# The sums of the first product's x blocks: added by VectorE in place of DMA, with new times for steps of the first and second product

## The chip, the cores and the metric

The kernel runs on one core of a Trainium2 chip. The metric is the device time of one execution in microseconds (us); lower is better. One profiled execution stands behind all rows of the trace.

## The reference

```python
x = attention(q, k, v)                   # causal, 2 batches, 12 heads, 448 tokens, head size 64
h = x @ w_in                             # x: 896 x 768, w_in: 768 x 2048
g = s * maximum(h, 0) ** 2 + b
x2 = g @ w_out                           # 2048 x 768
gate = 1 / (1 + exp(-(x2 @ w_gate)))     # 768 x 1536
out = ((gate * (x2 @ w_val)) @ w_out2)   # 1536 x 768
```

The weights arrive as 64-bit floats, and are read as pairs of 32-bit words.

## The kernel before, in words

**Stages.** Attention runs first, pair of heads by pair of heads, and leaves x in `x_b`: for each of six blocks of 128 features (k) and each of two batches (h) a tile of 128 x 448 for the high half and one for the low half (float32 split into two values that TensorE multiplies; x is their sum). Then come the first product (`w_in`, 16 feature blocks f), the second (`w_out`), the gate and value products, and the last product. Every product is made of three matmuls for each block: high by high, high weight by low x, low weight by high x. They stand in that order in `mm3`, so the third matmul of a product is the first that needs the weight's low half.

**The first product** has two parts. Feature blocks 0 to 7 are plain (`fill`: 18 matmuls for one f and one h). Blocks 8 to 15 are taken in four groups of two by a scheme with seven products in place of eight (class `Seven`, `early7`): it multiplies sums of weight blocks (`ab`, `s12`, `s34`, `d`) by sums and differences of x's blocks (`t1` to `t4`). Those differences need x in float32. `halves_of(k0, h)` is three blocks of a buffer `r_b` of 128 x 1344 elements for one quarter of x; `X11`, `X12`, `X21`, `X22` name the quarters. Before the change a quarter's high half is copied there by a DMA on SyncE's queue (`x_copy`, line 587), and its low half is added by an accumulating DMA on GpSimd's queue (`x_add`, line 591). Then `x_sum` makes a difference on VectorE (lines 599 and 601), `x_high` its high half on ScalarE (line 608) and `x_low` its low half on VectorE (line 611).

**A weight's way.** `load_words` (line 76) loads one piece of 768 KB into one of two raw buffers, by SyncE's queue. `float_steps` turns the pairs of words into float32 in four steps: one on ScalarE (line 87), two short ones on VectorE (lines 89 and 92), a long one on VectorE (line 97) and another (line 101), after which the raw buffer is free for the load after the next. `halves` makes the high half on ScalarE (line 114) and the low half either on VectorE by a subtraction (line 120) or, with `adder`, by a negating copy on ScalarE (line 117) and an accumulating DMA on GpSimd's queue (line 118).

**Order.** The order of instructions on each engine is written out by hand: `at(t, what, ...)` puts a step into a plan at time t, and the plan is emitted in order of t. The times only set the order; each engine works in order and waits where its operands are not there. One unit of plan time is nine matmuls. The plan's marks are X (start of the first product, first half of feature 0 done early), XQ = X + 32 (start of the seven-product scheme), Y = XQ + 28 (start of the second product), M = Y + 32 and 0 (start of the gate and value products, Y + 64). `PLAIN_LEAD[f]` says how long before its use feature f's weights are converted; `X_AT` holds the times of the steps on x's blocks, `OWN_1` and `OWN_2` those of the weights' steps in the seven-product schemes, `AFFINE_AT` and `G_AT` those of the steps that make the second product's input, `lead` the advance of the second product's weights. The first five features' conversions are taken one step at a time by `step` from one generator, `splits`. The load of a unit of weights is planned right behind the step that frees its raw buffer (`gone`).

The steps around the change, as the plan has them before:

```python
for i, n in enumerate((1, 0, 3, 2)):
    at(X + 1.5 + 2.2 * i, x_copy, n)
    at(X + 1.5 + 2.2 * i, x_add, n)
X_AT = (10.4, 11.07, 11.55, 14.31, 15, 15.6, 16.2, 17.5, 19, 20.06, 24.14, 26.97)
```

Of the kernel before, what the change touches and what calls it, by code (L numbers as in the profile page):

```python
# [13 lines left out]
ALU = mybir.AluOpType  # L14
U32 = mybir.dt.uint32
P = 128
# [8 lines left out]
def body(ctx: ExitStack, tc: tile.TileContext, qk, vp, w_in, w_outa, w_outb, s, b, w_gate, w_val, w_out2a, w_out2b, outT):  # L25
# [79 lines left out]
    def halves(tt, out, adder=False, name="w", slot=None):  # L105

        if slot is None:
            slot = turn("w", SLOTS, (1, 3, 0, 4, 2))
        hi = wp.tile([P, U, P], F32R, tag=f"{slot}h", name=f"{name}hi")
        lo = wp.tile([P, U, P], F32R, tag=f"{slot}l", name=f"{name}lo")  # L110
        out += [hi, lo]
        nn = tt.shape[1]
        hif, lof = (x.rearrange("p k m -> p (k m)")[:, :nn] for x in (hi, lo))
        nc.scalar.activation(out=hif, in_=f32(tt), func=AF.Copy)  # L114
        yield "dve"
        if adder:
            nc.scalar.activation(out=lof, in_=f32(hif), func=AF.Copy, scale=-1.0)  # L117
            nc.gpsimd.dma_start(out=lof, in_=f32(tt), accum_op=ALU.add)  # L118
        else:
            nc.vector.tensor_tensor(out=lof, in0=f32(tt), in1=f32(hif), op=ALU.subtract)  # L120

    def split_steps(raw, n, out):

        t = []
        yield from float_steps(raw, n, t)
        yield "act"
        yield from halves(t[0][:, :n * P], out)

    def mm3(acc, unit, K, x, h):

# [184 lines left out]
    def fill(f, h, k0, k1):  # L315
# [3 lines left out]
        wh, wl = split[f]  # L319
        mm3(acc[f, h], (wh[:, k0:k1], wl[:, k0:k1], k0, k1), KC, at_x, h)  # L320

    def splits():

        raw = load_words(w_in[0], KC)
        yield "act"
        for f in range(EARLY):
            now, raw = raw, load_words(w_in[f + 1], KC) if f + 1 < EARLY else None
            yield from split_steps(now, KC, split[f])
            yield "act"

    steps = splits()
# [208 lines left out]
    at(X + 0.9, step)  # L540
    at(X + 1.75, step)

    PLAIN_LEAD = (-0.15, -2.69, 0.73, 0.91, 1.15, 2.21, 2.47, 3.38)

    def plain_at(f):
        return X + PER * f - PLAIN_LEAD[f]
# [20 lines left out]

    for f in range(PLAIN):
        if f >= EARLY:
            split.append(unit(w_in[f], KC, plain_at(f), f"w{(1, 0, 4)[f - EARLY]}", f > EARLY))  # L570
        for h in range(B):
            t = X + (f + h / B) * PER
            if f == 0 and h == 0:
                at(t + 1.0, fill, 0, 0, KC // 2, KC)
            else:
                at(t, fill, f, h, 0, KC)
            timed(
                t + PER / B, (0.02, relu, lambda f=f, h=h: acc[f, h][:, :S], f, h), (0.35, square, f, h),
            )
# [2 lines left out]
    def halves_of(k0, h):  # L582
        return mem["rb"][:, B * k0 + h:B * (k0 + KH):B]

    def x_copy(n):
        k0, h = KH * (n // B), n % B
        nc.sync.dma_start(out=halves_of(k0, h), in_=f32(x_b[:, B * k0 + h:B * (k0 + KH):B, 0]))

    def x_add(n):
        k0, h = KH * (n // B), n % B  # L590
        nc.gpsimd.dma_start(out=halves_of(k0, h), in_=f32(x_b[:, B * k0 + h:B * (k0 + KH):B, 1]), accum_op=ALU.add)

    X11, X12, X21, X22 = ((0, 0), (0, 1), (KH, 0), (KH, 1))

# [15 lines left out]
    def x_low(ty, src):  # L610
        nc.vector.tensor_tensor(out=t_blocks(ty, 1), in0=halves_of(*src), in1=f32(t_blocks(ty, 0)), op=ALU.subtract)

    for i, n in enumerate((1, 0, 3, 2)):
        at(X + 1.5 + 2.2 * i, x_copy, n)
        at(X + 1.5 + 2.2 * i, x_add, n)
    X_AT = (10.4, 11.07, 11.55, 14.31, 15, 15.6, 16.2, 17.5, 19, 20.06, 24.14, 26.97)
    timed(
        X, (X_AT[0], x_sum, X11, X11, X12, ALU.subtract, False), (X_AT[1], x_high, "t1", X11),
        (X_AT[2], x_low, "t1", X11),
        (X_AT[3], x_sum, X12, X22, X12, ALU.subtract, False), (X_AT[4], x_high, "t3", X12),  # L620
        (X_AT[5], x_sum, X22, X11, X22, ALU.subtract, True), (X_AT[6], x_high, "t2", X22),
# [144 lines left out]
            3: ((1.05, add_r, q, f1), (1.40, relu_square, f1)),  # L766
        }[i]

    OWN_1 = {q: dict(zip(("g", "ab", "v", "s", "s12", "s34"), ts)) for q, ts in enumerate((((-10.2, -9.6, -8.8, -8.2), (-6.9, -6.3), (-7.7, -7.2, -6.6, -6.0), (-4.62, -4.32, -3.6, -3.3), (-2.58, -2.1), (-1.77, -0.68)), ((-4.23, -3.55, -2.65, -2.13), (-1.22, -0.46), (-1.56, -1.14, -0.54, -0.02), (0.38, 0.68, 1.4, 1.7), (3.49, 3.97), (3.23, 4.32)), ((2.77, 3.45, 4.35, 4.87), (6.29, 6.54), (5.32, 5.74, 6.34, 6.86), (7.38, 7.68, 8.4, 8.7), (9.32, 9.8), (10.23, 11.32)), ((9.77, 10.45, 11.35, 11.62), (13.26, 13.54), (12.32, 12.74, 13.34, 13.86), (14.38, 14.68, 15.4, 15.7), (16.12, 16.6), (17.23, 18.32))))}
    early7 = Seven(  # L770
        XQ, seq1, lambda q: tuple(w_in[f] for f in features(q)), OWN_1,
        lambda q: (f"w{1 - q % 2}", "w2", f"w{3 + q % 2}"), lambda n: mem["s1"][:, n % 4], first_x, evacuate_1,
# [14 lines left out]
    def g_time(k):  # L787
        return Y + 2 * k - G_AT[k]

    AFFINE_AT = (12.8, 14.6, 16.2, 17.8, 18.31, 21.0, 22.02, 24.83)  # L790
    G_AT = (3.0, 3.0, 3.0, 3.0, 3.0, 3.0, 3.0, 3.0, 4.93, 3.0, 2.34, 2.73, 2.95, 3.03, 1.1, 3.0)
    for k in range(PLAIN):
        for h in range(B):
            at(XQ + AFFINE_AT[k] + 0.8 * h, affine, k, h)
# [24 lines left out]
            )  # L819

    def lead(n):
        return (0.0, 0.0, 0.0, 0.0, 0.0, 0.63, 1.0, 1.64, 2.89, 3.64, 4.25, 5.0, 5.75, 7.45, 8.2, 8.95, 8.56)[n]

    for u in range(PIECES):
        w2.append(unit(w_outa[u], U, Y + PER * u - lead(u), f"w{W2[u]}"))
# [151 lines left out]
    seq = [(i, q) for i, q in seq if q < NF2]  # L977
    seq[-4:-2] = seq[-3], seq[-4]

    OWN_2 = {q: dict(zip(("g", "ab", "v", "s", "s12", "s34"), ts)) for q, ts in enumerate((((-15.6, -15.2, -14.5, -13.9), (-10.65, -9.8), (-13.3, -12.9, -12.3, -11.7), (-5.25, -4.95, -4.3, -4.0), (-4.6, -3.6), (-2.18, -1.97)), ((-11, -10.6, -10, -9.4), (-1.75, -1.25), (-8.9, -8.5, -7.9, -7.3), (-2.1, -1.8, 0.3, 0.6), (4.1, 5.09), (2.65, 3.1)), ((-6.38, -5.98, -5.12, -4.94), (5.78, 6.54), (5.32, 5.74, 6.34, 6.86), (7.38, 7.68, 8.4, 8.7), (9.32, 9.8), (10.23, 11.32))))}  # L980
    ring = {}

    def ringed(i, q):
# [193 lines left out]
```

## Time and profile before

| | |
|---|---|
| median of 3 runs | 556.46 us (555.77 to 559.13) |
| profiled execution | 556.3 us |
| its span, first to last instruction | 554.4 us |
| PE busy | 541.6 us (98%) |
| DVE busy | 430.6 us (78%) |
| ACT busy | 358.4 us (65%) |
| POOL busy | 91.2 us (16%) |
| granted TensorE clock, mean | 0.999 of full speed |

PE is TensorE's matmuls, PEld its weight loads, DVE VectorE, ACT ScalarE, POOL GpSimd, SP SyncE. A busy share is taken over the whole span. In a timeline a row is one instruction, or several alike in a run (x2); the bracket says how long its engine was idle just before it and what ended that. Times in the rows count from the span's start.

### The profile page before, as it was taken

The page shows a single profiled execution, that of the slowest core. Times are in us where ns is not written, and L with a number is a line of the kernel's source. Part 1 is how long each engine was busy: PE and PEld are TensorE (multiplying, and loading weights), DVE is VectorE, ACT ScalarE, POOL GpSimd, SP SyncE. Part 2 cuts the span into 40 slices and gives each one's busy share as a digit, 9 for nine tenths or more (in the row PEclk, how much of TensorE's full clock was granted, in tenths as well). Part 3 has the DMA queues.
Part 4 walks back from the last instruction along what each step waited for, and adds up shares of the span by engine and source line. Part 5 has one row for each costly group of instructions (what it writes and reads, how often), then busy time and mean ns, then how long its engine had stood idle before and what let it go on. Part 6 is the DMA issues. An engine that isn't in the chain of part 4 may idle for free.

```text
span 554.4 us, 8357 instructions
## 1 busy us (share of the span) xinstructions
PE 541.6 (98%) x3032; PEld 479.7 (87%) x3033; DVE 430.6 (78%) x783; ACT 358.4 (65%) x675; POOL 91.2 (16%) x147
## 2 busy tenths in 40 slices
PE   7999999899899999999999999999999999999997
PEld 3667789789799899999999999999999999999996
DVE  6899875689885899987789788888888999895300
ACT  7989945488789958954436777766767674734200
POOL 3667512101111000000000211121121210000000
PEclk9999999999999999999999999999999999999999
DMA  7846039787977334254345658888888863336000
GB/s 260 306 135 214 31 114 314 149 211 214 220 175 184 81 118 159 96 161 143 113 158 159 135 118 200 195 205 215 209 200 214 214 173 115 113 115 213 34 33 35
DMA packets 26425, 89.41 MB, mean 161 GB/s; under 512 B 2960, under 2 KB 10000, under 8 KB 26384
## 3 DMA queue, kind: packets, MB, share of 16 engines
q1 hardware_dynamic: 17152, 68.69, 34.9%
q0 software_dynamic: 8800, 19.27, 21.2%
q10 hardware_dynamic: 432, 0.92, 0.5%
q8 instruction: 24, 0.39, 0.3%
q14 instruction: 17, 0.14, 0.1%
HBM read 64.10 MB, written 2.75 MB: 121 GB/s over the span
## 4 chain that ended last, share of the span: by engine, by line
PE 65%; DMA 1%; ACT 0%; issue 0%; ACTq 0%
PE acc L135 18%; PE bankA L719 16%; PE acc L817 11%; PE bankC L719 8%; PE acc L1079 8%; PE bankE L719 4%; DMA d_w<-wt 1%; ACT ot L1092 0%; ACTq L1092 0%
## 5 line engine op out<-in xcount | busy, mean ns | idle before, releaser
L135 PE MATMUL acc<-x_b,whi 128*128 128x448 f32 x288 | 82.1, 366 | 0.9 <-ACT whi L114 0.9
L87 ACT ACTIVATE wt<-raw 128x768 f32<-128x768 f32 (+1 forms) x69 | 61.4, 890 | 24.0 <-DMA raw<-in_w_outb 8.2
L101 DVE SCALAR_TENSOR_TENSOR wt<-raw,wt 128x768 uint32<-128x768 uint32 (+1 forms) x69 | 65.6, 951 | 1.7
L97 DVE SCALAR_TENSOR_TENSOR wt<-raw,wt 128x768 uint32<-128x768 uint32 (+1 forms) x69 | 65.6, 950 | 1.3
L114 ACT ACTIVATE whi<-wt 128x768 fp32r<-128x768 f32 (+1 forms) x37 | 30.6, 826 | 44.1 <-DVE wt L101 41.1
L135 PEld LDWEIGHTS acc<-x_b,whi 128*128 128x128 f32 x288 | 53.9, 188 | 5.5 <-ACT whi L114 1.3
L89 DVE TENSOR_SCALAR wt<-wt 128x768 f32<-128x768 f32 (+1 forms) x69 | 38.6, 560 | 20.9 <-ACT wt L87 20.3
L135 PE MATMUL acc<-x_b,wlo 128*128 128x448 f32 x144 | 52.8, 367 | 1.8 <-DVE wlo L120 1.3
L213 ACT ACTIVATE pt<-pt,m 128x320 f32<-128x320 f32 (+6 forms) x84 | 41.7, 501 | 5.4 <-DVE m L210 5.3
L252 POOL TENSOR_SCALAR pt<-pt,r 128x128 f32<-128x128 f32 (+6 forms) x82 | 40.1, 510 | 27.7 <-DVE r L247 21.2
L120 DVE TENSOR_TENSOR wlo<-wt,whi 128x768 fp32r<-128x768 f32 (+1 forms) x35 | 33.1, 946 | 10.0 <-ACT whi L114 9.6
L92 DVE TENSOR_SCALAR wt<-wt 128x768 uint32<-128x768 uint32 (+1 forms) x69 | 38.5, 558 | 2.4
L118 POOL DMA_DIRECT2D ab_lo<-wt x16 | 13.8, 863 | 152.8 <-ACT ab_lo L117 118.5
L210 DVE CUSTOM_DVE_ANT_0 pt<-sc,mask 128x320 f32<-128x320 f32 (+6 forms) x84 | 30.4, 413 | 3.7 <-PE sc L223 3.4
L120 DVE TENSOR_TENSOR s_lo<-s,s_hi 128x768 fp32r<-128x768 f32 x16 | 15.3, 957 | 21.2 <-ACT s_hi L114 21.2
L135 PEld LDWEIGHTS acc<-x_b,wlo 128*128 128x128 f32 x144 | 27.0, 188 | 4.6 <-DVE wlo L120 1.7
L1092 ACT ACTIVATE ot<-acc 128x448 f32<-128x448 f32 x12 | 6.6, 546 | 36.2 <-PE acc L135 30.2
L114 ACT ACTIVATE s_hi<-s 128x768 fp32r<-128x768 f32 x32 | 26.7, 837 | 3.3 <-DVE s L661 3.3
L223 PE MATMUL sc<-qk 64*64 64x256 f32 (+6 forms) x336 | 24.9, 391 | 2.2 <-DMA qk<-in_qk 2.0
L118 POOL DMA_DIRECT2D s_lo<-s x16 | 13.8, 860 | 76.8 <-DVE wt L97 43.3
L294 PEld LDWEIGHTS po<-ptT,vt 128*64 128x64 f32 x192 | 12.6, 136 | 13.0 <-issue 9.4
L672 POOL DMA_DIRECT2D d_w<-wt x16 | 14.3, 897 | 57.9 <-ACT d_w L671 37.6
(214 smaller groups left out, 1433.5 us busy)
## 6 DMA issues: line engine op xcount, KB each, us to landing
raw<-in_w_in SPq DMA_DIRECT2D x16, 768.0 KB, 5.4
raw<-in_w_gate SPq DMA_DIRECT2D x12, 768.0 KB, 5.7
raw<-in_w_val SPq DMA_DIRECT2D x12, 768.0 KB, 5.9
ab_lo<-wt POOLq DMA_DIRECT2D x16, 384.0 KB, 5.7
s_lo<-s POOLq DMA_DIRECT2D x16, 384.0 KB, 4.8
raw<-in_w_outa SPq DMA_DIRECT2D x8, 768.0 KB, 4.2
qk<-in_qk SPq DMA_DIRECT2D x9, 608.0 KB, 5.1
raw<-in_w_out2a SPq DMA_DIRECT2D x6, 768.0 KB, 4.5
```

The costliest lines, as they stand in the source:

```text
L87: nc.scalar.activation(out=f32(tt), in_=f32(high), func=AF.Abs, scale=RAISE)
L89: nc.vector.tensor_scalar(out=f32(tt), in0=f32(tt), scalar1=F64_TINY, scalar2=F64_HUGE, op0=ALU.max, op1=ALU.min,)
L97: nc.vector.scalar_tensor_tensor(out=tt, in0=low, scalar=29, in1=tt, op0=ALU.logical_shift_right, op1=ALU.bitwise_or,)
L101: nc.vector.scalar_tensor_tensor(out=tt, in0=high, scalar=SIGN, in1=tt, op0=ALU.bitwise_and, op1=ALU.bitwise_xor,)
L114: nc.scalar.activation(out=hif, in_=f32(tt), func=AF.Copy)
L120: nc.vector.tensor_tensor(out=lof, in0=f32(tt), in1=f32(hif), op=ALU.subtract)
L135: nc.tensor.matmul(acc[:, :S], w[:, k - k0], m, start=k == 0 and i == 0, stop=k == K - 1 and i == 2)
L213: nc.scalar.activation(out=pc, in_=pc, func=AF.Exp, scale=-1.0, bias=m, accum_out=l)
L252: engine.tensor_scalar(out=probs(i, c), in0=probs(i, c), scalar1=st[i]["r"][:, c:c + 1], scalar2=1.0, op0=ALU.mult, op1=ALU.mult,)
L719: nc.tensor.matmul(acc[:, :S], a[:, j], m, start=fresh and j == 0 and n == 0, stop=j == KH - 1 and n == 2, skip_group_check=True,)
L817: nc.tensor.matmul(acc[:, :S], w[:, kk * GROUP + d], m, start=k == 0 and n == 0, stop=k == NF1 - 1 and n == 2,)
L1079: nc.tensor.matmul(acc[d, h][:, :S], w[:, k * GROUP + d], m, start=u == 0 and k == 0 and n == 0, stop=u == NF2 // 2 - 1 and k == 1 and n == 2,
```

## The change

`x_copy` and `x_add` go. In their place `x_whole` adds the two halves of a quarter of x on VectorE, at four times behind the others in `X_AT`. The other times of `X_AT` are set anew, most of them earlier. Feature 5's low half is now made with `adder` (`ADDED_EARLY`; features 6 and 7 had it before). `PLAIN_LEAD`, three entries of `OWN_1`, `AFFINE_AT`, `G_AT`, `lead` and three entries of `OWN_2` have new numbers.

```diff
--- before.py
+++ after.py
@@ -119,12 +119,12 @@
         else:
             nc.vector.tensor_tensor(out=lof, in0=f32(tt), in1=f32(hif), op=ALU.subtract)
 
-    def split_steps(raw, n, out):
+    def split_steps(raw, n, out, adder):
 
         t = []
         yield from float_steps(raw, n, t)
         yield "act"
-        yield from halves(t[0][:, :n * P], out)
+        yield from halves(t[0][:, :n * P], out, adder)
 
     def mm3(acc, unit, K, x, h):
 
@@ -319,13 +319,15 @@
         wh, wl = split[f]
         mm3(acc[f, h], (wh[:, k0:k1], wl[:, k0:k1], k0, k1), KC, at_x, h)
 
+    ADDED_EARLY = (False, False, False, False, False, True, True, True)
+
     def splits():
 
         raw = load_words(w_in[0], KC)
         yield "act"
         for f in range(EARLY):
             now, raw = raw, load_words(w_in[f + 1], KC) if f + 1 < EARLY else None
-            yield from split_steps(now, KC, split[f])
+            yield from split_steps(now, KC, split[f], ADDED_EARLY[f])
             yield "act"
 
     steps = splits()
@@ -540,7 +542,7 @@
     at(X + 0.9, step)
     at(X + 1.75, step)
 
-    PLAIN_LEAD = (-0.15, -2.69, 0.73, 0.91, 1.15, 2.21, 2.47, 3.38)
+    PLAIN_LEAD = (0.23, -2.27, 1.15, 1.33, 1.09, 3.84, 2.14, 2.19)
 
     def plain_at(f):
         return X + PER * f - PLAIN_LEAD[f]
@@ -567,7 +569,7 @@
 
     for f in range(PLAIN):
         if f >= EARLY:
-            split.append(unit(w_in[f], KC, plain_at(f), f"w{(1, 0, 4)[f - EARLY]}", f > EARLY))
+            split.append(unit(w_in[f], KC, plain_at(f), f"w{(1, 0, 4)[f - EARLY]}", ADDED_EARLY[f]))
         for h in range(B):
             t = X + (f + h / B) * PER
             if f == 0 and h == 0:
@@ -582,13 +584,9 @@
     def halves_of(k0, h):
         return mem["rb"][:, B * k0 + h:B * (k0 + KH):B]
 
-    def x_copy(n):
-        k0, h = KH * (n // B), n % B
-        nc.sync.dma_start(out=halves_of(k0, h), in_=f32(x_b[:, B * k0 + h:B * (k0 + KH):B, 0]))
-
-    def x_add(n):
-        k0, h = KH * (n // B), n % B
-        nc.gpsimd.dma_start(out=halves_of(k0, h), in_=f32(x_b[:, B * k0 + h:B * (k0 + KH):B, 1]), accum_op=ALU.add)
+    def x_whole(k0, h):
+        hi, lo = (f32(x_b[:, B * k0 + h:B * (k0 + KH):B, n]) for n in range(2))
+        nc.vector.tensor_tensor(out=halves_of(k0, h), in0=hi, in1=lo, op=ALU.add)
 
     X11, X12, X21, X22 = ((0, 0), (0, 1), (KH, 0), (KH, 1))
 
@@ -610,12 +608,10 @@
     def x_low(ty, src):
         nc.vector.tensor_tensor(out=t_blocks(ty, 1), in0=halves_of(*src), in1=f32(t_blocks(ty, 0)), op=ALU.subtract)
 
-    for i, n in enumerate((1, 0, 3, 2)):
-        at(X + 1.5 + 2.2 * i, x_copy, n)
-        at(X + 1.5 + 2.2 * i, x_add, n)
-    X_AT = (10.4, 11.07, 11.55, 14.31, 15, 15.6, 16.2, 17.5, 19, 20.06, 24.14, 26.97)
+    X_AT = (5, 5.65, 7.57, 9.24, 10, 11.5, 12.37, 18.22, 14.98, 16, 19.03, 22, 1.77, 3.2, 6.7, 12.59)
     timed(
-        X, (X_AT[0], x_sum, X11, X11, X12, ALU.subtract, False), (X_AT[1], x_high, "t1", X11),
+        X, (X_AT[12], x_whole, *X12), (X_AT[13], x_whole, *X11), (X_AT[14], x_whole, *X22), (X_AT[15], x_whole, *X21),
+        (X_AT[0], x_sum, X11, X11, X12, ALU.subtract, False), (X_AT[1], x_high, "t1", X11),
         (X_AT[2], x_low, "t1", X11),
         (X_AT[3], x_sum, X12, X22, X12, ALU.subtract, False), (X_AT[4], x_high, "t3", X12),
         (X_AT[5], x_sum, X22, X11, X22, ALU.subtract, True), (X_AT[6], x_high, "t2", X22),
@@ -766,7 +762,7 @@
             3: ((1.05, add_r, q, f1), (1.40, relu_square, f1)),
         }[i]
 
-    OWN_1 = {q: dict(zip(("g", "ab", "v", "s", "s12", "s34"), ts)) for q, ts in enumerate((((-10.2, -9.6, -8.8, -8.2), (-6.9, -6.3), (-7.7, -7.2, -6.6, -6.0), (-4.62, -4.32, -3.6, -3.3), (-2.58, -2.1), (-1.77, -0.68)), ((-4.23, -3.55, -2.65, -2.13), (-1.22, -0.46), (-1.56, -1.14, -0.54, -0.02), (0.38, 0.68, 1.4, 1.7), (3.49, 3.97), (3.23, 4.32)), ((2.77, 3.45, 4.35, 4.87), (6.29, 6.54), (5.32, 5.74, 6.34, 6.86), (7.38, 7.68, 8.4, 8.7), (9.32, 9.8), (10.23, 11.32)), ((9.77, 10.45, 11.35, 11.62), (13.26, 13.54), (12.32, 12.74, 13.34, 13.86), (14.38, 14.68, 15.4, 15.7), (16.12, 16.6), (17.23, 18.32))))}
+    OWN_1 = {q: dict(zip(("g", "ab", "v", "s", "s12", "s34"), ts)) for q, ts in enumerate((((-10.2, -9.6, -8.8, -8.2), (-6.9, -6.3), (-7.7, -7.2, -6.6, -6.0), (-4.62, -4.32, -3.6, -3.3), (-3.68, -3.2), (-1.77, -0.68)), ((-4.23, -3.55, -2.65, -2.13), (-0.6, 0.16), (-1.56, -1.14, -0.54, -0.02), (0.38, 0.68, 1.4, 1.7), (3.68, 4.16), (3.23, 4.32)), ((2.77, 3.45, 4.35, 4.87), (6.29, 6.54), (5.5, 5.72, 6.74, 7.26), (7.38, 7.68, 8.4, 8.7), (9.32, 9.8), (10.23, 11.32)), ((9.77, 10.45, 11.35, 11.62), (13.26, 13.54), (12.32, 12.74, 13.34, 13.86), (14.38, 14.68, 15.4, 15.7), (16.12, 16.6), (17.23, 18.32))))}
     early7 = Seven(
         XQ, seq1, lambda q: tuple(w_in[f] for f in features(q)), OWN_1,
         lambda q: (f"w{1 - q % 2}", "w2", f"w{3 + q % 2}"), lambda n: mem["s1"][:, n % 4], first_x, evacuate_1,
@@ -787,8 +783,8 @@
     def g_time(k):
         return Y + 2 * k - G_AT[k]
 
-    AFFINE_AT = (12.8, 14.6, 16.2, 17.8, 18.31, 21.0, 22.02, 24.83)
-    G_AT = (3.0, 3.0, 3.0, 3.0, 3.0, 3.0, 3.0, 3.0, 4.93, 3.0, 2.34, 2.73, 2.95, 3.03, 1.1, 3.0)
+    AFFINE_AT = (12.95, 13.73, 16.2, 17.8, 18.31, 21.0, 22.02, 26.11)
+    G_AT = (3.0, 3.0, 3.0, 3.0, 3.0, 3.12, 3.95, 3.0, 5.36, 3.42, 2.34, 2.73, 2.95, 3.03, 1.1, 3.0)
     for k in range(PLAIN):
         for h in range(B):
             at(XQ + AFFINE_AT[k] + 0.8 * h, affine, k, h)
@@ -819,7 +815,7 @@
             )
 
     def lead(n):
-        return (0.0, 0.0, 0.0, 0.0, 0.0, 0.63, 1.0, 1.64, 2.89, 3.64, 4.25, 5.0, 5.75, 7.45, 8.2, 8.95, 8.56)[n]
+        return (0.0, 0.0, 0.0, 0.0, 0.0, 0.63, 1.0, 1.64, 2.89, 4.63, 4.25, 5.99, 5.75, 7.31, 8.2, 8.95, 8.56)[n]
 
     for u in range(PIECES):
         w2.append(unit(w_outa[u], U, Y + PER * u - lead(u), f"w{W2[u]}"))
@@ -977,7 +973,7 @@
     seq = [(i, q) for i, q in seq if q < NF2]
     seq[-4:-2] = seq[-3], seq[-4]
 
-    OWN_2 = {q: dict(zip(("g", "ab", "v", "s", "s12", "s34"), ts)) for q, ts in enumerate((((-15.6, -15.2, -14.5, -13.9), (-10.65, -9.8), (-13.3, -12.9, -12.3, -11.7), (-5.25, -4.95, -4.3, -4.0), (-4.6, -3.6), (-2.18, -1.97)), ((-11, -10.6, -10, -9.4), (-1.75, -1.25), (-8.9, -8.5, -7.9, -7.3), (-2.1, -1.8, 0.3, 0.6), (4.1, 5.09), (2.65, 3.1)), ((-6.38, -5.98, -5.12, -4.94), (5.78, 6.54), (5.32, 5.74, 6.34, 6.86), (7.38, 7.68, 8.4, 8.7), (9.32, 9.8), (10.23, 11.32))))}
+    OWN_2 = {q: dict(zip(("g", "ab", "v", "s", "s12", "s34"), ts)) for q, ts in enumerate((((-15.6, -15.2, -14.5, -13.9), (-10.65, -9.8), (-13.3, -12.9, -12.3, -11.7), (-5.25, -4.95, -4.3, -4.0), (-3.68, -2.68), (-1.82, -1.6)), ((-11.11, -10.71, -10.11, -9.51), (-1.75, -1.25), (-8.9, -8.5, -7.9, -7.3), (-2.1, -1.8, 0.3, 0.6), (4.1, 5.09), (2.65, 3.1)), ((-6.38, -5.98, -5.12, -4.94), (5.78, 6.54), (5.32, 5.74, 6.34, 6.86), (7.38, 7.68, 8.4, 8.7), (9.32, 9.8), (10.23, 11.32))))}
     ring = {}
 
     def ringed(i, q):
```

## Rows read from the trace of the kernel before

**Rows 1.** the chain that ended last: start us, us, what, matmuls

```profile
192.88 58.37 PE acc L817 x288
```

**Rows 2.** timeline of PE, 77 to 193 us: start us, us, instruction [idle before <-releaser]

```profile
77.56 0.67 PE L135 MATMUL acc<-x_b,whi 128*128 128x448 f32 x2
...
106.12 0.68 PE L135 MATMUL acc<-x_b,whi 128*128 128x448 f32 x2 [0.92 <-ACT whi L114]
108.13 0.47 PE L135 MATMUL acc<-x_b,wlo 128*128 128x448 f32 x1 [1.33 <-DVE wlo L120]
...
122.41 0.57 PE L135 MATMUL acc<-x_b,whi 128*128 128x448 f32 x2
123.43 0.47 PE L135 MATMUL acc<-x_b,wlo 128*128 128x448 f32 x1 [0.45 <-DMA wlo<-wt]
...
137.71 0.57 PE L719 MATMUL bankA<-x_b,ab_hi 128*128 128x448 f32 x2
...
142.57 0.67 PE L719 MATMUL bankA<-t_b,s_hi 128*128 128x448 f32 x2 [1.06 <-ACT bankE L729]
...
144.50 0.57 PE L719 MATMUL bankE<-x_b,ab_hi 128*128 128x448 f32 x2
...
150.01 0.47 PE L719 MATMUL bankA<-x_b,ab_lo 128*128 128x448 f32 x1 [1.30 <-DMA ab_lo<-wt]
...
182.54 0.57 PE L719 MATMUL bankC<-x_b,s_hi 128*128 128x448 f32 x2
...
189.36 1.69 PE L719 MATMUL bankA<-t_b,d_w 128*128 128x448 f32 x7 [0.46 <-DMA d_w<-wt]
...
192.71 0.56 PE L817 MATMUL acc<-t_b,whi 128*128 128x448 f32 x2
```

**Rows 3.** timeline of DVE, 78 to 104 us, same columns

```profile
78.99 0.96 DVE L120 TENSOR_TENSOR wlo<-wt,whi 128x768 fp32r<-128x768 f32 x1
79.87 0.55 DVE L89 TENSOR_SCALAR wt<-wt 128x768 f32<-128x768 f32 x1
...
82.05 0.96 DVE L101 SCALAR_TENSOR_TENSOR wt<-raw,wt 128x768 uint32<-128x768 uint32 x1
...
93.20 0.96 DVE L97 SCALAR_TENSOR_TENSOR wt<-raw,wt 128x768 uint32<-128x768 uint32 x1
101.62 1.56 DVE L601 TENSOR_TENSOR r_b<-r_b 128x1344 f32<-128x1344 f32 x1 [7.46 <-DMA r_b<-x_b]
103.10 0.95 DVE L101 SCALAR_TENSOR_TENSOR wt<-raw,wt 128x768 uint32<-128x768 uint32 x1
```

**Rows 4.** timeline of SP's queue, 60 to 200 us: DMA issues

```profile
89.14 0.33 SPq L76 DMA_DIRECT2D raw<-in_w_in  x1
...
104.11 50.60 SPq L76 DMA_DIRECT2D raw<-in_w_in  x10
```

**Rows 5.** line 591, the accumulating DMA of x: issue to landing

```profile
DMA to landing us min/median/max: 6.9/8.0/8.7
```

**Rows 6.** line 118, the accumulating DMA of a weight's low half: issue to landing

```profile
DMA to landing us min/median/max: 3.9/4.8/8.6
```

**Rows 7.** line 76, the loads of weights: issue to landing

```profile
DMA to landing us min/median/max: 4.0/4.7/8.5
```

**Rows 8.** timeline of ACT, 103 to 142 us, columns as in rows 2

```profile
103.22 1.33 ACT L608 ACTIVATE t_b<-r_b 128x1344 fp32r<-128x1344 f32 x1 [7.77 <-DVE r_b L601]
...
138.73 0.85 ACT L114 ACTIVATE ab_hi<-wt 128x768 fp32r<-128x768 f32 x1
...
141.99 0.53 ACT L729 ACTIVATE bankE<-bankA 128x448 f32<-128x448 f32 x1
```

**Rows 9.** timeline of DVE, 239 us, the second product's last low halves

```profile
239.49 1.17 DVE L785 TENSOR_TENSOR g_a<-r_b,g_a 128x448 fp32r<-128x448 f32 x2 [0.34 <-ACT g_a L781]
```

**Rows 10.** windows: us, busy (x) of PE, PEld, DVE, ACT, POOL; PEclk, DMA, GB/s

```profile
75.00:100.00 25.00, 25.00 (x131) 22.21 (x130) 14.17 (x18) 10.76 (x17) 2.77 (x2) 1.00 0.89 260
...
125.00:150.00 25.00, 22.66 (x111) 20.34 (x109) 23.26 (x32) 20.38 (x34) 5.09 (x6) 1.00 0.83 218
```

## What I predict

> **What bounds the kernel now.** I read the page first: PE is busy 98% of a span of 554.4 us, and the profiled execution took 556.3 us, so 1.9 us lie around the span; the median of the runs, 556.46, is the same within what I can tell. A kernel that waits only a few us on PE can win only those, so the next views are the chain that ended last and PE's timeline. In the chain the second product is one piece of 288 matmuls in 58.37 us [rows 1], 0.2027 us a matmul. A unit of work (nine matmuls, the plan's unit of time) is therefore 1.824 us. From 192.88 us to the end the chain is PE in pieces of that pace, so nothing that this change does there can gain.
>
> Before it, PE's starts tell where time is lost [rows 2]. I count units from 77.56, where the second half of feature 0 begins (X + 1 in the plan). Feature 6 begins 23 units later, which at full pace is 119.51; it begins at 122.41, so 2.90 us were lost, around the two waits at 106.12 (high half of feature 4's weights) and 108.13 (its low half). The first group of the seven-product scheme, 31 units on, is due at 134.10 and begins at 137.71: 0.71 more, at feature 6's low half, which comes by DMA. The bankE product, 34 units on, is due at 139.58 and begins at 144.50: 1.31 more, the copy of bankA into bankE being late. At 54 units (due 176.06, begun 182.54) it is 1.56 more, at the low half of group 1's `ab` weights. At 59 units (due 185.18, begun 192.71) it is 1.05 more, mainly at `d_w`. Together 7.53 us, and each wait costs some 0.2 more than its idle column says, since the first matmuls after it start at a wider pitch.
>
> Then the cause of the largest. VectorE sat idle 7.46 us before the first block difference at 101.62, waiting for the DMAs that add x's low half to its high half [rows 3]. Those additions take 6.9 to 8.7 us each to land [rows 5] and start only when their copies have landed. VectorE works in order, so the next instruction behind that difference, feature 4's last step of conversion, ran at 103.10 instead of about 94.2, right after the step before it at 93.20. The high half, the low half and feature 4's matmuls followed. The same step frees the raw buffer that feature 6's load needs: SyncE issued one load at 89.14 and the next at 104.11 [rows 4]. From there the loads, of which only two can be under way, run back to back, and the later three waits are on weights that came late.
>
> **The change part by part.** Removed: four copies on SP's queue, four accumulating DMAs on POOL's, and VectorE's wait for them. On SP the loads no longer stand behind copies; they still wait for raw buffers.
>
> Added: four additions of 1344 float32 elements on VectorE. The trace has none from `x_b`; the nearest row is the difference of the same size, two inputs in SBUF, 1.56 us [rows 3]. An instruction that does not need the one before it begins 0.08 before that one's end, as at 78.99 and 79.87, so one costs 1.48 in a queue. The bounds are 1.48 and 1.56; I take 1.48, since its neighbours in the order don't need it. Nothing excludes that the strided operands cost a little less, but 0.2 us over three of them is all that is at stake.
>
> Also: feature 5's low half goes from VectorE (0.96) to a negating copy on ACT (a 768-element copy there takes 0.85 [rows 8]) and an accumulating DMA, 3.9 to 8.6 us to landing [rows 6].
>
> Now the new order on VectorE, from 78.99, by plan times, with 0.88 for a 768-element subtraction, 0.58 + 0.48 for the two short steps, 1.00 or 0.88 for each long step (1.00 when the next one needs it), 1.48 for each 1344-element operation. Feature 1's low half, feature 2's steps with the sums X12 and X11 between and behind them, feature 2's low half: 0.88 + 1.06 + 1.48 + 1.00 + 0.88 + 1.48 + 0.88 = 7.66, so 86.65. Feature 3 with the first difference, X22 and the low half of `t1`: 1.06 + 1.48 + 1.00 + 0.88 + 1.48 + 1.48 + 0.88 = 8.26, so 94.91. Feature 4 woven with feature 5 and two differences: 1.06 + 1.48 + 0.88 + 1.06 + 0.88 + 0.88 + 1.48 + 0.88, then feature 4's low half, 0.96: 9.56, so it ends at 104.47. PE needs it for the third matmul of feature 4: 77.56 + 15 units = 104.92, plus 0.1 for the start and 0.41 for two matmuls, 105.43. The margin is 1.0 us where before there was a wait. Features 2 and 3 have 3 us or more. The additions ahead of feature 4 (three, 4.44 us) fill idle time: VectorE works only 14.17 of the 25 us from 75 to 100 [rows 10].
>
> What must be there in time. Feature 5's load is issued when feature 3's conversion is done, about 91.2 (before: 89.14); with the median landing of 4.7 [rows 7] it is there at 95.9, its first ACT step ends at 96.8, and VectorE wants it at 98.4. Feature 5's halves on ACT stand behind the high half of `t2` (1.33 [rows 8]) and end about 105.8; its DMA lands 3.9 to 5.8 us later, by 111.6 at the latest, and PE wants it at 112.6. What is queued behind POOL's new wait for ACT is only later DMAs of the same kind.
>
> Feature 6's load leaves at about 101.2 instead of 104.11, and its conversion ends about 111 instead of 116.8. Its DMA goes out at about 113, lands at 117 to 119, and PE wants it at 119.9: the 0.71 goes. In the same way group 1's first conversion (group 0's is done by 127) ends about 132.6, before 138.4. Its `ab` high half ran at 138.73 and held back the copy into bankE until 141.99 [rows 8]; now it ends by 133.9, and the copy begins when its product ends, with 1.1 us in hand: the 1.31 goes. The low half of that `ab` then leaves at 135.4 and, even behind another of its kind, lands by 142 against a need at 143.6: the 1.56 goes. The 1.05 behind it hangs on ACT's own queue from 161 us on and on the landing of one DMA beside a load; the new times of four affine steps leave the sum of ACT's work before it the same, so I leave it.
>
> The new times in the second product change the order by one or two instructions. Engines run ahead of the plan there: the last low halves are made at 239.49 [rows 9] and PE wants them at 192.71 + 29 units = 245.6 or later. I cost them at nothing; the cover is those 5 us, and without it each moved step would cost its own length, 0.6 to 0.9.
>
> Sum: 2.90 + 0.71 + 1.31 + 1.56 = 6.48, less 0.1 of start that stays, 6.4. 556.3 - 6.4 = 549.9.
>
> **The rivals.** Feature 5 comes late. If its load lands after 8.5 us, the longest [rows 7], its first step ends at 100.6, 2.2 after VectorE wants it; feature 4's low half stands behind it, so 1.2 beyond the margin, 1.3 with the restart: 551.2. For it: the margin is thin; against: the long landings fell beside other transfers, and x's are gone.
>
> Order, not lateness, makes the waits at bankE and `ab`. Then 1.31 + 1.56 stay: 552.8. For it: ACT is full from 136 to 142 us; against: its first late step waited for a conversion.
>
> Only the wait at feature 4 goes, because loads through two raw buffers set the pace anyway: 556.3 - 2.8 = 553.5. Against it: the ring has had a gap of 15 us (89.14 to 104.11), which closes.
>
> Everything before 193 us goes: 556.3 - 7.5 = 548.8, or 548.5 with 0.3 of refills.
>
> Slower: VectorE becomes the bound. It is busy 23.26 of 25 us from 125 to 150 [rows 10], and gets 5.0 us more (4 x 1.48 less 0.88). If the three additions ahead of feature 4 find none of the idle time, because the first waits for something that ends no sooner than the DMAs did, feature 4's low half comes 4.44 later than now: 560.7. It decides from where less than 4.4 us of the 7.46 can be used. Against it: x's last low half is ready before 78.99 and the idle time lies ahead of the very instruction that waited. The Trainium skill's page "Perfetto Trace Analysis", section "Optimizing Scalar/DVE Operations", says that work should be taken off VectorE when it is saturated; the change puts work on it, and by that rule the time would be the 560.7. The row of 75 to 100 us speaks against the rule here: VectorE isn't saturated where the additions go.
>
> **How the numbers follow.** Forecast 549.9: 0.55. Feature 5 late, 551.2: 0.15. Order, 552.8: 0.14. Only feature 4, 553.5: 0.06. Everything, 548.5: 0.05. Slower: 0.05. The range from 548.5 to 552.8 takes in all but the last of the gains and the loss, with some tenths of scatter at its ends. About 1% is what a measurement here can tell from no change, 550.9 from the median: faster 0.55 + 0.05 = 0.60, the same 0.35, slower 0.05.
>
> **What would show it.** After the change no VectorE wait of several us before the first difference, three additions of about 1.5 us before 93 us, no PE wait at feature 4, loads issued without the 15 us gap, the second product beginning at about 186.3. A PE wait on feature 4's low half would mean that the margin was counted wrong; waits at bankE or `ab` that order makes them; a wait within the second product that its new times cost something.

## The result and the profile after

Over 22 runs of each kernel, the changed kernel's median is 551.94 us (549.55 to 559.65) and that of the kernel before 556.52 us (555.34 to 564.66). The ratio is 0.9917, with a 95% interval from 0.9893 to 0.994: 0.8% faster. I had forecast 549.9, with a range from 548.5 to 552.8. The profiled execution took 551.66 us with a span of 549.9. Executions more than 1.5% above the fastest of their kernel are in the medians, but not in the ratios.

Two profiled executions differ already before the change's place: the second half of feature 0 begins at 77.56 before and at 76.88 after, and in the ten profiles of the experiments below, whose attention is the same, between 76.49 and 77.43. That is scatter. So I compare the stretch from there to the second product, 59 units or 107.6 us at full pace; measured to the second product's entry in the chain (192.88 before [rows 1]), which stands 0.17 behind its first matmul, 107.79. Before, it took 192.88 - 77.56 = 115.32. The chain that ended last in the changed kernel (start, duration, what):

```profile
187.67 58.37 PE acc L813 x288
```

187.67 - 76.88 = 110.79: 4.5 us less. I had forecast 6.4 less, 108.9. The rest of the span nearly cancels: this execution begins the stretch 0.7 us earlier, and takes 0.7 more behind it, 362.2 (549.9 - 187.67) where it was 361.5 (554.4 - 192.88). The timeline of PE after, at the places of [rows 2]:

```profile
76.88 0.67 PE L135 MATMUL acc<-x_b,whi 128*128 128x448 f32 x2
...
104.35 0.56 PE L135 MATMUL acc<-x_b,whi 128*128 128x448 f32 x2
104.75 0.37 PE L135 MATMUL acc<-x_b,wlo 128*128 128x448 f32 x1
...
118.94 0.57 PE L135 MATMUL acc<-x_b,whi 128*128 128x448 f32 x2
...
133.53 0.57 PE L715 MATMUL bankA<-x_b,ab_hi 128*128 128x448 f32 x2
...
139.01 0.57 PE L715 MATMUL bankE<-x_b,ab_hi 128*128 128x448 f32 x2
144.86 0.47 PE L715 MATMUL bankA<-x_b,ab_lo 128*128 128x448 f32 x1 [1.64 <-DMA ab_lo<-wt]
184.16 1.69 PE L715 MATMUL bankA<-t_b,d_w 128*128 128x448 f32 x7 [0.62 <-DMA d_w<-wt]
...
187.50 0.56 PE L813 MATMUL acc<-t_b,whi 128*128 128x448 f32 x2
```

Feature 4 begins at 104.35, due (15 units from 76.88, and 0.1 for the start) at 104.34, and its third matmul, the first that needs the low half, follows 0.40 later with no wait. Feature 6 (118.94), the first product of the seven-product scheme (133.53) and bankE's product (139.01) are on time within 0.02. So three of the four waits that I expected to go have gone. The fourth has not: at 144.86 the low half of group 1's `ab` weights still makes PE wait, with an idle time of 1.64 where it was 1.30. The wait on `d_w` at 184.16, which I had left in, is 0.62, before 0.46. The view of PE's waits (total, times, longest) shows a third:

```profile
PE bankA L715 <- DMA ab_lo<-wt: 1.6, 1, 1.6
...
PE bankA L715 <- ACT r_f L985: 0.9, 1, 0.9
PE bankA L715 <- DMA d_w<-wt: 0.6, 1, 0.6
```

The one on `r_f` is late, at 445 us, in the gate and value products, which the change reaches only by times for the first groups.

VectorE after, at the places of [rows 3]:

```profile
80.25 1.55 DVE L589 TENSOR_TENSOR r_b<-x_b 128x1344 f32<-128x1344 f32 x1
...
83.58 1.55 DVE L589 TENSOR_TENSOR r_b<-x_b 128x1344 f32<-128x1344 f32 x1
...
86.98 1.55 DVE L599 TENSOR_TENSOR r_b<-r_b 128x1344 f32<-128x1344 f32 x1
...
90.32 1.55 DVE L589 TENSOR_TENSOR r_b<-x_b 128x1344 f32<-128x1344 f32 x1
...
98.59 0.95 DVE L101 SCALAR_TENSOR_TENSOR wt<-raw,wt 128x768 uint32<-128x768 uint32 x1
...
102.66 0.95 DVE L120 TENSOR_TENSOR wlo<-wt,whi 128x768 fp32r<-128x768 f32 x1
103.53 1.55 DVE L589 TENSOR_TENSOR r_b<-x_b 128x1344 f32<-128x1344 f32 x1
```

The additions (line 589) take 1.55 each, and one starts 1.47 before its follower, as reckoned. The first difference at 86.98 no longer waits. Feature 4's last step runs at 98.59 (before: 103.10) and its low half ends at 103.61; my sum, shifted by the 0.68 by which this execution is earlier, said 103.79. PE wants it at 104.75: the margin is 1.1 us. SyncE's queue no longer holds copies of x between the loads, so the view draws all of them as one row; read in narrower windows, they leave at 90.47, 99.61 and 102.82, and the longest gap up to feature 6's load is 9.1 us where it was 15.0 [rows 4]:

```profile
76.91 71.82 SPq L76 DMA_DIRECT2D raw<-in_w_in  x13
```

Two more things show in these traces. The loads also land sooner: the five that left from 77 to 110 us took 4.8 to 6.5 us before, beside x's DMAs, and the seven that leave from 76 to 116 now take 4.1 to 4.3. Feature 6's load, which left at 104.11 and took 6.5, now leaves at 99.61 and takes 4.2; counted from the start of the stretch it is there 6.1 us earlier, 3.8 by the raw buffer and 2.3 by the landing. And VectorE is nearly full where the additions went: from 75 to 100 us it is busy 23.91 of the 25 us, where it was 14.17 [rows 10].

### The profile page after: what moved, and what is told of

It reads as the page before. It is cut to its first block, busy times and chain, and to the rows that moved or that the text cites. A ratio compares the mean times of both kernels' runs of the same rounds, so it can differ in the third digit from the quotient of the medians.

```text
span 549.9 us, 8352 instructions
## 1 busy us (share of the span) xinstructions
PE 540.6 (98%) x3032; PEld 480.0 (87%) x3033; DVE 434.5 (79%) x786; ACT 359.0 (65%) x676; POOL 86.4 (16%) x144
## 4 chain that ended last, share of the span: by engine, by line
PE 62%; DMA 2%; DVE 1%; ACT 1%; issue 1%; ACTq 0%; SPq 0%
PE acc L135 19%; PE bankA L715 14%; PE acc L813 11%; PE acc L1075 8%; PE bankC L715 7%; PE bankE L715 3%; DMA raw<-in_w_out2a 1%; DMA d_w<-wt 1%; DVE wt L101 0%; DVE wt L89 0%; DVE r_f L992 0%; DVE wt L97 0%; ACT wt L87 0%; ACT s_hi L114 0%; ACT whi L114 0%
## 5 line engine op out<-in xcount | busy, mean ns | idle before, releaser
L223 PE MATMUL sc<-qk 64*64 64x64 f32 (+6 forms) x336 | 25.1, 394 | 1.3 <-DMA qk<-in_qk 1.2
L662 ACT ACTIVATE d_w<-wt 128x384 fp32r<-128x384 f32 x16 | 8.4, 523 | 23.6 <-PE bankA L715 23.6
```

## The experiments

All ten were profiled, and timed beside the kernel before on the same chip. "Stretch" is the time from the second half of feature 0 to the second product, as above; it leaves out the scatter of attention and of what comes later. The latter is large: in four of the profiles (additions alone, without the tables of later steps, ab of group 1 on VectorE, feature 5 on VectorE) each half of the last product takes 44.64 us, in the eight others 43.78. The additions alone, and the changed kernel:

```profile
459.00 44.64 PE acc L1074 x216
```

```profile
458.75 43.78 PE acc L1075 x216
```

The slower pace begins at about 445 us, makes no wait, and costs such an execution some 2 us; the granted clock of 460 to 500 us reads 1.00 in all twelve. The cause stays open. So a difference of 2 us between two profiled times, or between medians of a few runs, need not come from the edit. The medians are also of several sets of runs; each ratio is to the runs of the kernel before in the same set.

| kernel | median us | ratio to before (95%) | stretch us |
|---|---|---|---|
| before | 556.52 | 1 | 115.32 |
| changed | 551.94 | 0.9917 (0.9893 to 0.994) | 110.79 |
| changed, again | 550.63 | 0.9869 (0.9814 to 0.9925) | 110.30 |
| additions alone | 551.52 | 0.99 (0.9873 to 0.9927) | 109.73 |
| without the tables of later steps | 553.17 | 0.9915 (0.9893 to 0.9937) | 111.01 |
| changed, ab of group 1 on VectorE | 549.25 | 0.9865 (0.9844 to 0.9885) | 108.87 |
| two more additions | 553.6 | 0.9934 (0.9911 to 0.9957) | 112.67 |
| additions alone, ab on VectorE | 549.57 | 0.9838 (0.9794 to 0.9881) | 109.05 |
| DMA kept, order alone | 557.11 | 0.998 (0.9947 to 1.0012) | 114.93 |
| changed, ab and d on VectorE | 548.51 | 0.9825 (0.9777 to 0.9873) | 107.89 |
| additions alone, ab and d on VectorE | 548.58 | 0.9832 (0.9781 to 0.9884) | 107.93 |
| changed, feature 5 on VectorE | 552.41 | 0.9898 (0.9862 to 0.9934) | 110.56 |

My theory: VectorE's in-order queue waited for the DMAs of x ahead of feature 4's conversion, and through the raw buffers that made the later weights late. Rivals: order alone is to blame; the new times carry the gain; VectorE is the bound.

**The additions alone.** The kernel before with the engine changed and nothing else (the definition of `x_whole` is that of the change):

```diff
-        at(X + 1.5 + 2.2 * i, x_copy, n)
-        at(X + 1.5 + 2.2 * i, x_add, n)
+        at(X + 1.5 + 2.2 * i, x_whole, KH * (n // B), n % B)
```

> The kernel before with nothing but the change of engine: the four additions on VectorE at the plan times at which the copies and the accumulating DMAs stood (X + 1.5, 3.7, 5.9, 8.1), all other times and feature 5's low half as before. Theory (the wait of VectorE's queue for the DMAs is the cause of the loss at feature 4 and, through the raw buffers, of the later ones): counted with the steps of the prediction, feature 4's low half ends some 4 us before PE wants it, no PE wait at features 4 and 6, time 549.9 to 551.5 (a gain of 5 to 6.5). Rival (the new times are what makes the additions fit): the wait at feature 4 goes but waits at feature 6, bankE or the ab weights stay, 553.5 to 555. Second rival (VectorE is the bound): slower than 556.

Its ratio, 0.99, is that of the whole change; its median is at the upper end of what I expected. VectorE's timeline at feature 4's low half, and PE's waits after attention:

```profile
101.37 0.95 DVE L120 TENSOR_TENSOR wlo<-wt,whi 128x768 fp32r<-128x768 f32 x1
```

```profile
PE bankA L714 <- ACT r_f L984: 1.4, 1, 1.4
...
PE bankA L714 <- DMA d_w<-wt: 0.6, 1, 0.6
PE bankA L714 <- DMA ab_lo<-wt: 0.4, 1, 0.4
```

The low half ends at 102.32 and PE, which begins feature 0's second half at 77.43 here, wants it at 105.3. The margin was 3 us, not the 4 that I counted: VectorE waited 0.41 for feature 3's first step and 0.53 for ScalarE's half of a difference. The rival of the new times falls: the change of engine by itself removes the waits at features 4 and 6 and at bankE. It leaves 0.4 on `ab` and 0.6 on `d_w`; the wait on `r_f` is the late one again. The stretch, 109.73, is even 0.6 to 1.1 shorter than in the two profiles of the changed kernel: counted from its start, the DMA of `ab` leaves at 58.44 (there 59.13 and 58.84) and takes 8.2 us (there 8.8 and 8.7). With one profile that is a hint, not a proof, that the new times cost a little there.

**Without the tables of later steps.** The changed kernel with the tables OWN_1, AFFINE_AT, G_AT, lead and OWN_2 of before, which bear on the seven-product schemes and the second product (one of the five is shown):

```diff
-    AFFINE_AT = (12.95, 13.73, 16.2, 17.8, 18.31, 21.0, 22.02, 26.11)
+    AFFINE_AT = (12.8, 14.6, 16.2, 17.8, 18.31, 21.0, 22.02, 24.83)
...
```

> The changed kernel with the five tables of OWN_1, OWN_2, AFFINE_AT, G_AT and lead as they were before: the additions, feature 5's low half by DMA, X_AT and PLAIN_LEAD of the change alone. Theory (the new times of the second product and of the seven-product schemes are covered by engines that run 5 us ahead): the same as the changed kernel within 0.7 us, with the wait on group 1's ab weights present. Rival (those times hold a part of the gain): 1 us or more slower than the changed kernel, with a wait at bankE or in the second product.

The stretch is 111.01 against 110.79 and 110.30 in the two executions of the changed kernel, and the ratios are the same, 0.9915 and 0.9917. The new times of those steps are worth nothing that shows. OWN_1, which changes in four entries and not in three, also holds the times of group 1's `ab`, which the change sets 0.6 units later: by the old ones its low half leaves right behind that of `s34`, 0.64 us apart instead of 1.66. POOL's timeline, and the DMAs issued from 132 to 138 us (count, KB, landing):

```profile
135.08 0.85 POOL L118 DMA_DIRECT2D s_lo<-s  x1 [3.28 <-ACT s_lo L117]
135.72 1.07 POOL L118 DMA_DIRECT2D ab_lo<-wt  x1
```

```profile
s_lo<-s POOLq DMA_DIRECT2D x1, 384.0 KB, 4.7
ab_lo<-wt POOLq DMA_DIRECT2D x1, 384.0 KB, 9.0
```

135.72 + 9.0 = 144.7. With the new times the pair is this, and a load (`raw`) lies beside it:

```profile
134.35 0.85 POOL L118 DMA_DIRECT2D s_lo<-s  x1 [2.54 <-DVE wt L92]
136.01 0.83 POOL L118 DMA_DIRECT2D ab_lo<-wt  x1 [0.81 <-ACT ab_lo L117]
```

```profile
raw<-in_w_in SPq DMA_DIRECT2D x1, 768.0 KB, 6.7
ab_lo<-wt POOLq DMA_DIRECT2D x1, 384.0 KB, 8.8
```

136.01 + 8.8 = 144.8. Setting them further apart let the second one land no earlier here.

**Group 1's ab on VectorE.** One low half of the changed kernel by a subtraction:

```diff
-            t["ab"] = parted(tg, KC, times["ab"], ab, True, "ab_")
+            t["ab"] = parted(tg, KC, times["ab"], ab, not (self.base == XQ and q == 1), "ab_")
```

> The changed kernel with the low half of group 1's ab weights subtracted on VectorE (0.96 us) in place of the negating copy and the accumulating DMA. Theory (the 2.0 us pitch at 144.86 in the changed kernel is the landing of that DMA, 8.8 us behind another accumulation and beside a load): the wait goes, 1.8 to 2.0 us faster than the changed kernel, about 549.8. Rival (group 1's conversion is late, whichever engine makes the low half): the wait stays, now on VectorE, and the time is the same within 0.7.

```profile
136.14 0.95 DVE L120 TENSOR_TENSOR ab_lo<-wt,ab_hi 128x768 fp32r<-128x768 f32 x1
```

```profile
PE bankA L715 <- DMA d_w<-wt: 0.6, 1, 0.6
```

The subtraction runs at 136.14, about when the DMA left in the changed kernel, and is done at 137.1, some 6 us before PE wants it. The wait is gone, and after attention only `d_w` stays. The stretch is 108.87: 1.9 less than the profile of the changed kernel, 1.4 less than its second. The conversion was in time; the way by the copy and the DMA was not, and 8.8 us of it are the landing.

**Two more additions.** X11 added three times in the changed kernel (cut from one long line):

```diff
-(X_AT[13], x_whole, *X11),
+(X_AT[13], x_whole, *X11), (3.21, x_whole, *X11), (3.22, x_whole, *X11),
```

> The changed kernel with the addition of one quarter of x (X11) done three times instead of once: 2.96 us more on VectorE ahead of feature 4's low half, with the same values. Theory (VectorE's queue sets when that half is ready, with a margin of 1.1 us): a PE wait of about 1.8 us on it at feature 4, and the time 0 to 2 us above the changed kernel, since the later wait on the ab weights shrinks as PE comes later. Rival (other things than VectorE's queue set it, the DMA of feature 5 for one): no wait at feature 4. Rival (VectorE is the bound from here on): 3 us slower or more.

VectorE's and PE's timelines:

```profile
83.84 4.74 DVE L589 TENSOR_TENSOR r_b<-x_b 128x1344 f32<-128x1344 f32 x3
...
106.10 0.95 DVE L120 TENSOR_TENSOR wlo<-wt,whi 128x768 fp32r<-128x768 f32 x1
```

```profile
107.11 0.47 PE L135 MATMUL acc<-x_b,wlo 128*128 128x448 f32 x1 [1.85 <-DVE wlo L120]
```

The three additions run in 4.74, 3.19 more than the one, feature 4's low half starts at 106.10, and PE waits 1.85 for it (expected 1.8): the margin was 1.1 and VectorE's queue sets that time. The stretch is 1.9 to 2.4 above the changed kernel's, at the upper end of what I expected or over it: the wait on `ab` shrank, but only to 1.0.

**Order alone.** The kernel before with x still added by DMA, and only three steps moved behind feature 4's:

```diff
-    X_AT = (10.4, 11.07, 11.55, 14.31, ...
+    X_AT = (12.1, 12.2, 12.9, 14.31, ...
```

> The kernel before with x added by DMA as it was, and only the first difference, its high half and its low half moved in the plan from X + 10.4, 11.07, 11.55 to 12.1, 12.2, 12.9, behind feature 4's conversion. Theory (the DMAs themselves are too slow, not only their place in VectorE's queue): the wait at feature 4 goes, but the second difference still waits for its DMA until 109.7 us and feature 6's conversion stands behind it, so its low half lands at 123.4 as before against a need at 119.9; PE waits 3 to 3.6 us there, and the time stays at 555 to 557. Rival (the order was the whole cause, and the engine of the additions does not matter): 549.5 to 552.

Its timelines of VectorE, POOL and PE:

```profile
97.05 0.95 DVE L120 TENSOR_TENSOR wlo<-wt,whi 128x768 fp32r<-128x768 f32 x1
102.60 1.56 DVE L601 TENSOR_TENSOR r_b<-r_b 128x1344 f32<-128x1344 f32 x1 [4.60 <-issue]
...
108.80 1.56 DVE L601 TENSOR_TENSOR r_b<-r_b 128x1344 f32<-128x1344 f32 x1 [0.82 <-DMA r_b<-x_b]
...
114.79 0.96 DVE L101 SCALAR_TENSOR_TENSOR wt<-raw,wt 128x768 uint32<-128x768 uint32 x1
```

```profile
118.19 0.88 POOL L118 DMA_DIRECT2D wlo<-wt  x1 [7.83 <-ACT wlo L117]
```

```profile
122.20 0.47 PE L135 MATMUL acc<-x_b,wlo 128*128 128x448 f32 x1 [2.58 <-DMA wlo<-wt]
```

Feature 4's low half now runs at 97.05 and PE does not wait for it. But the first difference waits until 102.60 (the view names no releaser; the second DMA of its two quarters left at 92.97 and took 9.5 to land), the second until 108.80, feature 6's conversion ends at 115.75, its DMA leaves at 118.19, and PE waits 2.58 at 122.20 where it waited 0.45. The ratio is 0.998, no change. The wait was moved, not removed: for this order the rival falls, and with it the thought that the loss at feature 4 was worth 2.9 us by itself. The size was a little under my 3 to 3.6. An order that also puts feature 6's conversion ahead of the second difference was not tried, so it is not shown that no order would do with the DMAs kept.

**The changed kernel again.**

> The changed kernel once more, beside the others of this call, for their comparison and for a second profile. Theory (the PE wait of 1.0 us at 445 us in its first profile is the chance landing of a load, since the same code after 310 us showed 1.5 us in the kernel with the additions alone and none with group 1's low half on VectorE): about 552, the wait on the ab weights 1.7 to 2.0 again, the one at 445 of another size. Rival (the new times make it): the wait at 445 is 1.0 us again.

The DMA wait on `ab` is 1.2, and at 445 us the view lists none. Kernels with the same late code show there anything from no wait to 1.6; PE's row in this execution, 0.3 behind where the pitch of the matmuls before it would put it:

```profile
444.12 0.88 PE L715 MATMUL bankA<-x_a,d_w 128*128 128x448 f32 x3
```

In the changed kernel's profile, ScalarE's step on a load of the last product waited 2.18 for that load, and behind it stood the copy that frees bankA:

```profile
441.21 0.93 ACT L87 ACTIVATE wt<-raw 128x768 f32<-128x768 f32 x1 [2.18 <-DMA raw<-in_w_out2a]
...
445.14 0.52 ACT L985 ACTIVATE r_f<-bankA 128x448 f32<-128x448 f32 x1
```

The loads of that stage (two of `w_out2a`, median us to landing), in the changed kernel's profile, in this one, and in the kernel with feature 5 on VectorE, where PE waited 1.6:

```profile
raw<-in_w_out2a SPq DMA_DIRECT2D x2, 768.0 KB, 7.9
```

```profile
raw<-in_w_out2a SPq DMA_DIRECT2D x2, 768.0 KB, 6.6
```

```profile
raw<-in_w_out2a SPq DMA_DIRECT2D x2, 768.0 KB, 8.7
```

With landings of 7.9 and 8.7 PE waited 0.87 and 1.6 us, with 6.6 only 0.3. The kernel with the additions alone waited 1.4; the kernel before, with the same late code, has no such wait in its list. So the code does not decide it. Why loads land slower in some executions stays open.

**The additions alone, with ab on VectorE.** The edit of the additions alone, and the one of `ab`:

```diff
+        at(X + 1.5 + 2.2 * i, x_whole, KH * (n // B), n % B)
...
+            t["ab"] = parted(tg, KC, times["ab"], ab, not (self.base == XQ and q == 1), "ab_")
```

> The kernel before with the additions on VectorE at the plan times of the copies and DMAs, as in the run with the additions alone, and group 1's ab low half on VectorE; no new times, feature 5 as before. Theory (the new times and feature 5's move are worth nothing beside these two): as fast as the changed kernel with group 1's low half on VectorE, 549.0 to 550.5. Rival (the new times hold a part of the gain once the ab wait is gone): 551 or more, with waits that the other has not.

The stretch is 109.05 against 108.87 with the new times, so they carry nothing here either.

**Feature 5 on VectorE.** The other half of the question about feature 5:

```diff
-    ADDED_EARLY = (False, False, False, False, False, True, True, True)
+    ADDED_EARLY = (False, False, False, False, False, False, True, True)
```

> The changed kernel with feature 5's low half subtracted on VectorE, as it was before the change, instead of the negating copy and the accumulating DMA. Theory (VectorE has room there, and feature 5 is needed 7 us after feature 4): the same as the changed kernel within 0.5 us, 550.5 to 552, no wait at features 4 to 7, the ab wait of 1.2 to 1.9 us still there. Rival (VectorE is full after feature 4, and 0.88 us more delays the conversions of features 6, 7 and the groups): a larger wait on the ab weights or a new one, 0.8 us or more slower.

The stretch is 110.56, between the two executions of the changed kernel, with no wait at features 4 to 7. The median is 0.5 above the changed kernel's and over my 552. That says little: its profile is one of the four with the slower last product, and holds the largest wait of all at 446 us:

```profile
PE bankA L715 <- ACT r_f L985: 1.6, 1, 1.6
```

Moving feature 5's low half to the DMA gained nothing that shows, and cost nothing.

**Both ab and d on VectorE.** The changed kernel, with group 3's `d` too:

```diff
+            src = f32(self.quads[q]["tt"][1][0][:, KH * P:])
+            if self.base == XQ and q == 3:
+                nc.vector.tensor_tensor(out=lo, in0=src, in1=f32(hi), op=ALU.subtract)
+                return
             nc.scalar.activation(out=lo, in_=f32(hi), func=AF.Copy, scale=-1.0)
...
```

> The changed kernel with the low half of group 1's ab weights and that of group 3's d weights subtracted on VectorE in place of a negating copy and an accumulating DMA. Theory (the PE wait at 184 us is the 6.1 us landing of d_w's DMA beside a load): that wait goes too, 0.7 to 0.9 us less than with group 1's alone, about 548.4. Rival (ScalarE's queue makes d late, whichever engine makes the low half): the wait stays, 549.2.

```profile
175.01 0.56 DVE L669 TENSOR_TENSOR d_w<-wt,d_w 128x384 fp32r<-128x384 f32 x1 [0.56 <-ACT d_w L662]
```

```profile
181.10 1.98 PE L719 MATMUL bankA<-t_b,d_w 128*128 128x448 f32 x9
```

The subtraction runs at 175.01, and the nine matmuls on `d_w` from 181.10 on run as one piece. The stretch, 107.89, is full pace within 0.1. ScalarE's place for the high half by itself did not make PE wait: that step starts 97.4 us into the stretch with or without this edit (with only `ab` on VectorE, 174.76 - 77.32). What made PE wait is the way of the low half behind it: there, 1.2 us from the high half's end through the negating copy to the DMA's leaving, and 6.1 to its landing. No run parts the two.

**The same without any new time.** The kernel before with the additions, `ab` and `d` on VectorE, and every time as it was:

```diff
+        at(X + 1.5 + 2.2 * i, x_whole, KH * (n // B), n % B)
...
+            if self.base == XQ and q == 3:
+                nc.vector.tensor_tensor(out=lo, in0=src, in1=f32(hi), op=ALU.subtract)
+                return
...
+            t["ab"] = parted(tg, KC, times["ab"], ab, not (self.base == XQ and q == 1), "ab_")
```

> The kernel before with three engine changes and no new time at all: the additions of x on VectorE at the plan times of the copies and DMAs, the low half of group 1's ab weights and that of group 3's d weights subtracted on VectorE. Theory (the new times and feature 5's move carry nothing): no PE wait between 77 us and the second product over 0.3 us, the time of the changed kernel with the same two low halves on VectorE, 548 to 549.5. Rival (the new times hold something that shows once the other waits are gone): a wait at bankE or feature 6, 550 or more.

```profile
PE cold L354 <- DVE warm L348: 1.2, 1, 1.2
PE sc L223 <- DMA qk<-in_qk: 1.1, 1, 1.1
PE cold L354 <- issue: 0.2, 1, 0.2
```

These are all the waits of PE that the view lists, and all lie in attention or ahead of it. The stretch is 107.93, the median 548.58 against 548.51. This is the plainest version that beats both kernels: three changes of engine, 1.7% under before.

## Why the prediction was right, and where it was off

**The cause.** Right for feature 4, the largest: VectorE's queue waited for x's DMAs, and the rows show the wait, the step behind it, and both gone. The additions alone give the gain, and the one order tried with the DMAs kept gives none. For feature 6 and bankE the raw buffers passed the delay on, as forecast, but the loads also landed sooner once x's DMAs were gone, which the prediction names only against a rival and does not count; no run parts the two.

**Feature 4, 2.90, and feature 6, 0.71.** Both went. The sum along VectorE's queue was off by 0.2 us over 25 us, the margin by 0.1, and two more additions used it up as counted.

**bankE, 1.31.** Went, for the reason given.

**Group 1's ab, 1.56.** This term failed, in the step "even behind another of its kind, lands by 142 against a need at 143.6". Two numbers were off. It left at 136.01, which is 1.3 later than my 135.4 in this execution's time; and it landed after 8.8 us, when I had allowed 6.6 at most. The row of 8.6 was in my rows [rows 6], and it came from this very DMA before the change, behind the same `s34` and beside a load. I left it out of the sum; but being on time changes nothing in what lies beside it. In all eight profiles that have this DMA it took 7.7 to 9.0. So 1.8 were lost there again instead of nothing, about the whole shortfall of 1.9 in the stretch (6.4 forecast, 4.5 measured). The rival "order, not lateness" named this wait and was half right: for `ab`, not for bankE. The median lies between its 552.8 and the forecast's 549.9. That the profiled time misses the forecast by 1.8, just what `ab` cost, is in part luck: 0.7 won before the stretch pays for 0.7 lost behind it.

**What was left in, 1.05.** It stayed at about 1.0. The kernels with `d` on VectorE show that it need not have.

**The second product at nothing.** Right within what the profile can tell: no PE wait there in any of the kernels.

**Slower, VectorE the bound.** Falls: the additions fit into idle time with 1.1 us to spare, and two more cost at feature 4 what goes beyond that, 1.85 of the 3.19 that they took, not their length. The two low halves put back on VectorE did not cost time either; they took 2.4 to 2.9 us off the stretch of the changed kernel and 1.8 off that of the additions alone. Where they went, the changed kernel has VectorE busy 19.75 of the 25 us from 125 to 150 and 10.31 of the 12 from 175 to 187. The Trainium skill, "Perfetto Trace Analysis", section "Optimizing Scalar/DVE Operations", says that moving some work off VectorE may make sense if it is saturated. These runs do not speak against that, since its condition did not hold in the stretches where the work was put; after the change, at 23.91 of 25 us, it nearly holds from 75 to 100.

**The chances.** I gave 0.60 to a gain of over 1%. The median is 0.8% under before; the wait on `ab` that stayed makes up the difference: without it the ratio is 0.9865.

## What to carry to other kernels

An engine that works in order and waits for a chain of DMAs delays everything behind it, and a ring of load buffers hands that delay on; in the one order tried here, moving the waiting step only moved the wait, while making the value on the engine that waits for it removed both. A long landing in a trace may belong to what runs beside the transfer (here that is argued; no run took the neighbours away): before leaving it out of a sum, ask whether its neighbours will still be there when everything is on time. Where runs scatter by a per cent, a stretch of one profile between two fixed points of the busiest engine tells what medians cannot, down to about half a microsecond (the two profiles of the changed kernel are 110.79 and 110.30).

## What the runs showed of the hardware that was not expected

An accumulating DMA of 384 KB that was issued 0.64 to 1.67 us behind another of the same size took 7.7 to 9.0 us to land in all eight profiles that have the pair, and the first of the two 3.9 to 4.7. The distance did not matter to tenths that can be told apart: at 0.64 to 0.68 the second took 8.2 to 9.0, at 1.66 to 1.67 7.7 to 8.8.

The loads of 768 KB that left up to 110 us landed in 4.8 to 6.5 us beside x's DMAs, and in 4.1 to 4.3 without them.

The last product's halves of 216 matmuls ran in 44.64 us in four executions and in 43.78 in eight, at a granted clock that the rows give as 1.00 in both.
